# Key-value sums in 32-column strips and a new order of all jobs, in a one-core linear-attention and mixer kernel

## The chip, the core and the metric

The program runs on one core of one Trainium2 chip. The core has TensorE (PE), VectorE (DVE), ScalarE (ACT), GpSimd (POOL) and SyncE (SP), each with its own instruction stream; they meet through semaphores. PE reads SBUF and writes PSUM, which here is one tile `banks` of eight banks of 512 float32 columns. The metric is the device time of one execution in microseconds (us), as the median of several runs.

## What is computed

With x of 2048 tokens and 448 features, everything in bfloat16 and xn = layernorm(x), the output is x + A(xn) + B(xn).

```
q, k, v = split(xn @ wqkv)               # 16 heads of 28
pq, pk  = q @ w_phi, k @ w_phi           # per head
phi_q   = concat(softmax(pq), softmax(-pq));  phi_k the same of pk
kv, z   = phi_k^T @ v, sum_s phi_k       # per head, over all tokens
A = (phi_q @ kv) / (phi_q @ z + 1e-6) @ wo
h = gelu(layernorm(xn) @ w1); four column groups of h shifted by +1, -1, +2, -2 tokens
x1 = xn + shifted(h) @ w2
B = x1 + gelu(layernorm(x1) @ w3) @ w4
```

## The kernel before, in words

**Recording and order.** Nothing is issued while the Python code runs. `Recorder` (from L19) collects every operation with the memory that it reads and writes; `solve` (L76) works out which semaphore each must wait for, and `emit` plays one list per engine. All matmuls have the line L204, all ScalarE operations L212, most VectorE and GpSimd operations L216. So the order on each engine is the order of the calls, and that is written out by hand in two lists: the jobs of `chain` (L960 to L981) and the pairs of `play` (L1046 to L1068).

**Tiling.** There are 16 token tiles of 128 tokens. The 448 features are cut into overlapping chunks, so that most matmuls use 64 rows of the array. Lower rows (0 to 63, `LO`) and upper rows (64 to 127, `HI`) hold different weights and write different banks; `row_pairs` (L530) interleaves one of each. A matmul of 64 rows and 128 weight columns is in the profile as 64*128, its moving operand as, for example, 64x448. `Recorder._tile` (L198) notes the row division; on a change of division `solve` makes PE wait for its own last matmul on the same bank.

**The chain (prologue).** Layernorm statistics on VectorE (`"m"`), the inverse root on ScalarE (`"q"`) or GpSimd (`"r"`), the apply on VectorE (`"a"`) or GpSimd (`"p"`), PE transposes of xn (`XT`, L208), value projections (`ZV`), w1 products (`ZW`, `ZH`), the leftover columns of w1 (`ZR`), the folding of w_phi into w_qkv (`FO`), and dummy matmuls on a constant (`HD`, `spin`). `chain` (L562) plays the lower half of each job at once and puts the upper half into a queue that follows 400 columns behind. A "zip" job gives one half four chunks and the other three; `odd` alternates which. At its end stand the first key, query and w2 products (`HF`).

**The list after it.** `k0`/`k1` and `q0`/`q1` are the key and query projections of two token tiles (two PE halves each) with ScalarE exponentials behind; `kn` is `k_norm` (a VectorE reduction and a reciprocal), `kx` is `k_product` (the GpSimd product of phi_k, L723). `w0`/`w1_` are the w2 products, with VectorE additions behind (`w2_out`). `lo`, `sc`, `A` and `G` are the second layernorm: statistics on VectorE, scale on GpSimd, apply (`g_apply`, on VectorE for the tiles in `on_dve`, else on GpSimd) and a DMA transpose on SP's queue into gT. `T` is the DMA transpose of the query exponentials; `a`/`b` are the two PE halves of a w3 pair (eight and six matmuls of 512 columns) with a Gelu behind that writes h3T, which lies over phi_k. `N` is the attention product of a tile with its VectorE and GpSimd division, `f` the four parts of the last products, `S` the store.

**Key-value sums.** `K` is `kv_tile` (L725): 16 matmuls a tile, eight pairs of a lower and an upper half, weights a block of phi_k (64 tokens by 128 columns), moving 59 columns of `vaug` (values with a column of ones); lower halves add up in bank 6 and upper halves in bank 7. `kv_copy` (L739) copies bank 6 and adds bank 7; `kv_blocks` (L744) gathers the diagonal blocks with four matmuls against the selection matrix `pick` and four copies of 32 partitions, two on VectorE and two on ScalarE, into `kvq`, which `num_tile` (L766) reads as moving operand.

Of the kernel before, what the change touches and what calls it, by code (L numbers as in the profile page):

```python
# [224 lines left out]
def bass_parallel_sum__linear_kernel_hedgehog__mixer_s_mlp__prompt_kernel(  # L225
# [17 lines left out]
    with es:  # L243
# [58 lines left out]
        kvT = view(w1_r, 512)  # L302
        kvf = view(w1_r, 512, F32, at=1024)
        pick = view(w1_r, 2 * 128, at=3072).rearrange("p (s c) -> p s c", s=2)
# [257 lines left out]
        def chain(jobs, lag, even):  # L562
            at, upper, seen = [0, 0], deque(), {}
            odd, left = False, sum(j[0] == "zip" for j in jobs)
# [37 lines left out]
            for kind, make, then, *mid in jobs:  # L602
# [12 lines left out]
                else:  # L615
                    for n, item in enumerate(make(LO, (0, 1, 3) if odd else (0, 1, 2, 3))):
                        if mid and n == mid[0][0]:
                            both(*mid[0][1][1:])
                        low(item)
# [3 lines left out]
                    left -= 1  # L623
                    odd = not odd and left > even
# [281 lines left out]
        fb = {(1, 0): 3, (1, 2): 1, (0, 0): 3, (0, 2): 1}  # L906
# [45 lines left out]
        def HF(p, n):  # L952
# [7 lines left out]
        chain([  # L960
            L(("m", 0), ("q", 0, 1)), do(load_wT, 0, (1, 2, 3)), L(("m", 1), ("q", 1, 1), ("a", 0), ("a", 1)), HD(3, 3),
            HD(6, 3), HD(3, 3), L(("m", 2)), XT(0, 0, 1, "ACT"), L(("q", 2, 1)), HD(6, 3), L(("m", 3), ("m", 4)),
            XT(1, 2, 1, "ACT"), L(("p", 2), ("q", 3, 1), ("q", 4, 1), ("a", 3)), HD(6, 3), HD(6, 3), ZV(0, EV(0, "ACT", 1)),
            L(("m", 5), ("m", 7)), ZV(1, EV(1, "ACT", 1)), XT(2, 4, 1, "ACT"), L(("p", 4)), ZH(2, 0),
            L(("q", 5, 1), ("p", 5), ("m", 6), ("r", 6, 1)), inside(1, ZH(1, 0), XT(3, 0, 1, "ACT")), ZV(2, EV(2, "ACT", 1)),
            L(("q", 7, 1)), inside(1, ZH(0, 0), XT(4, 0, 1, "ACT")), L(("a", 7)),
            inside(2, ZH(0, 1, EW(0, 0, 1)), XT(5, 6, 1, "2")), L(("m", 15)), inside(1, ZH(2, 1), XT(7, 0, 1, "DVE")),
            L(("p", 6), ("m", 14), ("r", 15, 1)), ZV(3, EV(3, "ACT", 1)), ZV(4, EV(4, "ACT", 1)),
            inside(2, ZH(1, 1, EW(0, 1, 2)), XT(6, 0, 1, "DVE")), L(("m", 12), ("r", 14, 1), ("m", 13), ("a", 14)),
            ZV(5, EV(5, "ACT", 1)), ZW(1, 0, EW(1, 0, 1)), L(("p", 15), ("r", 12, 1), ("a", 12), ("m", 8)),  # L970
            ZW(1, 1, EW(1, 1, 1)), ZW(1, 2, EW(1, 2, 1)), L(("r", 13, 1)), XT(12, 6, 1, "ACT"), XT(14, 2, 2, "DVE"),
            L(("p", 13), ("m", 11)), do(load_w2), L(("r", 8, 1), ("p", 8)), ZV(7, EV(7, "ACT", 1)), L(("m", 10)),
            ZV(6, EV(6, "ACT", 1)), L(("m", 9), ("r", 11, 1), ("r", 10, 1)), XT(13, 6, 1, "ACT"), ZV(15, EV(15, "ACT", 1)),
            L(("a", 11)), do(phi_blocks), L(("a", 10)), ZV(14, EV(14, "ACT", 1)), ZW(3, 0, EW(3, 0, 1)),
            ZV(13, EV(13, "ACT", 1)), XD(11), XD(10), XT(8, 3, 1, "2"), FO(1, 2, 0), ZW(3, 2, EW(3, 2, 1)), FO(1, 0, 0),
            do(load_w3, 0), FO(1, 2, 1), ZW(3, 1, EW(3, 1, 1)), L(("r", 9, 1)), FO(1, 0, 1), ZV(12, EV(12, "ACT", 1)),
            ZV(8, EV(8, "ACT", 1)), L(("p", 9)), inside(3, ZR(0, 6, (rest_out, 0, 6), (rest_T, 0)), XT(9, 3, 1, "2")),
            FO(0, 2, 0), FO(0, 0, 0), FO(0, 2, 1), FO(0, 0, 1), ZV(9, EV(9, "DVE", 1)), do(late_3), do(h_shift, 0),
            ZR(1, 5, (rest_out, 1, 5)), do(kv_ones), ZV(11, EV(11, "ACT", 1)), HF(0, 0), ZW(2, 2, EW(2, 2, 1)), do(load_w4),
            ZW(2, 1, EW(2, 1, 1)), ZW(2, 0, EW(2, 0, 1)), ZV(10, EV(10, "DVE", 1)), HF(0, 1), HF(2, 0), HF(1, 0), HF(2, 1),  # L980
            do(h_shift, 1), do(kv_picks), HF(1, 1), do(rest_T, 1)], 400, 0)  # L981

        on_dve = (6, 8, 12)
# [42 lines left out]
        def A(i):  # L1026
            g_apply(i, dve if i in on_dve else pool)
# [75 lines left out]
```

## Time and profile before

| what | value |
|---|---|
| median of 3 runs | 171.19 us (171.19 to 171.23) |
| span of the profiled execution, first to last instruction | 169.2 us |
| what lies around it (median less span; the profiled execution's own total is not recorded) | 1.99 us |
| PE busy, matmuls | 165.9 us, 2359 |
| VectorE, GpSimd, ScalarE busy | 109.6, 92.2, 82.1 us |
| granted TensorE clock | 1.000 |

The span is the time between the first and the last instruction of the program. Busy times are those of the engines' instructions; a matmul's end is modelled, so that its duration contains the depth of the pipeline, and only the distance between starts tells how fast matmuls follow one another.

### The profile page before, as it was taken

Reading aid. Unit: us, or ns where it says so; the run is one execution under the profiler, and the core shown is the slowest. Engines: PE = TensorE matmul, PEld = TensorE weight load, DVE = VectorE, ACT = ScalarE, POOL = GpSimd, SP = SyncE. Lnnn points to the kernel's source line nnn. Section 1 sums busy time; section 2 is a strip of 40 time slices with the busy share of each in tenths; the row PEclk is TensorE's granted clock in tenths of the full one; section 3 lists DMA queues with packets and bytes.
Section 4 is the critical chain, followed back from the end, with each engine's and each line's share of the span. In section 5 each row is a group of like instructions: output and inputs, shape, how many; then the busy total and the mean of one; then the engine's idle time right before and its main releaser. Section 6 shows DMA issues by size and latency. Waiting matters only on the chain.

```text
span 169.2 us, 5423 instructions
## 1 busy us (share of the span) xinstructions
PE 165.9 (98%) x2359; PEld 99.3 (59%) x2359; DVE 109.6 (65%) x248; ACT 82.1 (49%) x110; POOL 92.2 (54%) x124
## 2 busy tenths in 40 slices
PE   8999999999999999999999999999999999999994
PEld 7776778667786555554554555555545555444453
DVE  3998866159999899929685896718617586220031
ACT  3599975797998878646242422024204041144000
POOL 5288980005999999951792264396730845404040
PEclk9999999999999999999999999999999999999999
DMA  5995579999599985671076664434554422310031
GB/s 162 364 197 103 98 135 293 164 330 149 99 141 183 278 97 149 86 134 27 7 118 127 95 135 55 84 73 42 135 68 93 59 61 62 83 60 4 0 109 54
DMA packets 50567, 19.93 MB, mean 118 GB/s; under 512 B 41712, under 2 KB 49840, under 8 KB 50544
## 3 DMA queue, kind: packets, MB, share of 16 engines
q1 hardware_dynamic: 49424, 18.71, 57.1%
q10 hardware_dynamic: 1120, 0.89, 1.6%
q8 instruction: 18, 0.29, 0.8%
q14 instruction: 5, 0.04, 0.1%
HBM read 7.14 MB, written 1.84 MB: 53 GB/s over the span
## 4 chain that ended last, share of the span: by engine, by line
PE 95%; DMA 1%; DVE 1%; issue 0%; DVEq 0%
PE banks L204 94%; DMA xtok<-in_A_x_dram 1%; PE banks L208 1%; DVE st L216 1%; DVE mv L216 0%; DVE xn L216 0%; DVE vaug L216 0%; DVEq L166 0%
## 5 line engine op out<-in xcount | busy, mean ns | idle before, releaser
L212 ACT ACTIVATE phik<-banks 128x1024 bf16<-128x1024 f32 (+1 forms) x44 | 42.2, 987 | 60.7 <-PE banks L204 60.5
L216 DVE TENSOR_TENSOR vaug<-banks,vaug 128x464 f32<-128x464 f32 (+3 forms) x65 | 32.8, 513 | 26.1 <-PE banks L204 24.5
L204 PE MATMUL banks<-gT,w 64*128 64x512 bf16 x392 | 48.2, 376 | 0.0
L204 PE MATMUL banks<-w,phik 64*128 64x448 bf16 (+3 forms) x434 | 45.2, 343 | 0.0
L216 POOL TENSOR_TENSOR xnT<-vaug 128x196 bf16<-128x196 f32 (+1 forms) x32 | 18.1, 587 | 29.6 <-DVE vaug L216 29.6
L204 PEld LDWEIGHTS banks<-w,phik 64*128 64x128 bf16 (+1 forms) x434 | 22.3, 94 | 20.1 <-issue 0.4
L204 PE MATMUL banks<-wv,xnT 64*128 64x448 bf16 (+2 forms) x222 | 32.9, 346 | 0.0
L723 POOL TENSOR_TENSOR phik<-phik,rks 128x1792 bf16<-128x1792 bf16 x8 | 25.6, 3219 | 8.5 <-DVE rks L216 8.5
L204 PEld LDWEIGHTS banks<-gT,w 64*128 64x128 bf16 x392 | 17.9, 94 | 18.0 <-ACT phik L212 0.4
L216 POOL TENSOR_TENSOR vaug<-xn,xtok 128x448 f32<-128x448 bf16 x16 | 16.2, 1034 | 12.7 <-DVE vaug L216 12.7
L204 PEld LDWEIGHTS banks<-wv,xnT 64*128 64x128 bf16 (+1 forms) x222 | 14.0, 94 | 7.7 <-PE banks L204 0.3
L204 PE MATMUL banks<-xnT,w 64*128 64x512 bf16 (+1 forms) x105 | 16.6, 334 | 0.0
L204 PE MATMUL banks<-wpk,xnT 64*128 64x448 bf16 x112 | 16.6, 349 | 0.0
L216 DVE TENSOR_REDUCE ksum<-phik 128x64 f32<-128x1792 bf16 x8 | 16.0, 2000 | 0.0
L204 PE MATMUL banks<-wpq,xnT 64*128 64x448 bf16 x112 | 15.7, 349 | 0.0
L212 ACT ACTIVATE hi<-banks 128x896 bf16<-128x896 f32 x16 | 13.7, 923 | 2.0 <-PE banks L204 2.0
L204 PE MATMUL banks<-w,hT 64*128 64x448 bf16 x96 | 13.6, 349 | 0.0
L216 POOL TENSOR_TENSOR rs<-mv,mhalf 128x1 f32<-128x1 f32 (+1 forms) x13 | 9.4, 727 | 6.2 <-DVE mv L216 6.0
L216 DVE RECIPROCAL vaug<-banks 128x16 f32<-128x16 f32 x16 | 4.0, 250 | 12.6 <-PE banks L204 12.6
L216 DVE TENSOR_TENSOR xn<-banks,xn 128x512 bf16<-128x512 f32 (+1 forms) x16 | 8.9, 598 | 2.3 <-PE banks L204 2.3
L216 POOL TENSOR_SCALAR g_tok<-xn,rs 128x512 bf16<-128x512 bf16 x13 | 9.9, 774 | 0.2
L216 DVE BATCH_NORM_STATS2 st<-xtok 128x6 f32<-128x448 bf16 x16 | 9.6, 601 | 0.2 <-DMA xtok<-in_A_x_dram 0.2
(67 smaller groups left out, 172.7 us busy)
## 6 DMA issues: line engine op xcount, KB each, us to landing
w<-in_B_w_dram SPq DMA_DIRECT2D x2, 896.0 KB, 5.8
out_dram<-vaug SPq DMA_DIRECT2D x15, 112.0 KB, 1.8
w<-in_B_w_dram SPq DMA_DIRECT2D x1, 1568.0 KB, 8.6
xtok<-in_A_x_dram SPq DMA_DIRECT2D x2, 448.0 KB, 6.3
wv<-in_A_wo_dram SPq DMA_DIRECT2D x2, 224.0 KB, 3.3
xtok<-in_A_x_dram SPq DMA_DIRECT2D x3, 112.0 KB, 3.6
xtok<-in_A_x_dram ACTq DMA_DIRECT2D x3, 112.0 KB, 4.2
w<-in_B_w_dram SPq DMA_DIRECT2D x1, 336.0 KB, 4.1
```

The lines of the kernel that those rows point to most:

```text
L204: self.op("PE", lambda e: e.matmul(out, lhsT, rhs, start=start, stop=stop, skip_group_check=True), [out], [lhsT, rhs], tile=self._tile(lhsT))
L208: self.op("PE", lambda e: e.transpose(out, in_, ident), [out], [in_, ident], tile=self._tile(in_))
L212: self.op("ACT", lambda e: e.activation(out, in_, func, **kw), [out], [in_] + aps)
L216: self.op(eng, lambda e: getattr(e, name)(out, *args, **kw), [out], aps)
L723: R.op(pool, lambda e: e.tensor_tensor(ph, ph, wide, op=ALU.mult), [ph], [ph, wide, *after])
```

## The change

The key-value sums change sides: `vaug` (30 columns of a head, all 128 tokens) becomes the weights and 64 columns of phi_k the moving operand. Each matmul's output lies in one of four strips of 32 PSUM partitions, which names one of four 32-column strips of the array. There are again 16 matmuls a tile, all in bank 6. One VectorE transpose in 32x32 blocks (`kv_turn`) and one product with a 0/1 mask (`kv_blocks`) then make `kvq`; the four gathering matmuls and the copies go. The 16 tiles are summed in five groups with no other PE work inside: (0, 4), (2, 5), (1, 3, 7, 11), (12, 13, 6, 10), (14, 8, 9, 15).

In `chain` a string of digits now tells for each zip job which half gets four chunks (1: the upper). The banks of value and w1 products are re-assigned and both lists are written anew. `AD` is the second layernorm's apply on VectorE, `A` on GpSimd. w2 is loaded at the front of the chain, the first half of w3 at its end, and wo just behind it. In the lists below only the new side is shown; the old one stands in the kernel above.

```diff
-        kvT = view(w1_r, 512)
-        kvf = view(w1_r, 512, F32, at=1024)
-        pick = view(w1_r, 2 * 128, at=3072).rearrange("p (s c) -> p s c", s=2)
+        kvT = view(w1_r, 256, F32)
+        pick = new("pick", 2, F32)
-        def chain(jobs, lag, even):
+        def chain(jobs, lag, heavy):
             at, upper, seen = [0, 0], deque(), {}
-            odd, left = False, sum(j[0] == "zip" for j in jobs)
+            turns = iter(heavy)
...
+                    odd = next(turns) == "1"
...
-                    left -= 1
-                    odd = not odd and left > even
...
         def kv_tile(i):
-            def side(k, rows):
-                return [(banks[6 + k][:, 64 * n:64 * n + VP + DH + 1],
-                         phik[rows[0]:rows[1], i, 4 * n:4 * n + 4, :].rearrange("p g e -> p (g e)"),
-                         vaug[rows[0]:rows[1], i, 2 * VP * n:2 * VP * n + VP + DH + 1]) for n in range(8)]
-            row_pairs(side(0, LO), side(1, HI), i == 0)
+            for n in range(4):
+                for j in range(4):
+                    h = 8 * (j // 2) + 2 * n + j % 2
+                    R.mm(banks[6][HP * j:HP * j + VP, 64 * n:64 * n + 64], vaug[:, i, VP * h:VP * h + VP],
+                         phik[:, i, 2 * h:2 * h + 2, :].rearrange("p g e -> p (g e)"), i == 0 and n == 0, False)
 
         def kv_picks():
-            R.ew(pool, "memset", pick[:, :, :], 0.0)
+            R.ew(pool, "memset", pick[:, :], 0.0)
             for q in range(4):
-                r = slice(HP * q, HP * q + HP)
-                R.ew(dve, "tensor_copy", pick[r, q % 2, :].rearrange("p (n e) -> p n e", n=4),
-                     ident[r, HP * q:HP * q + HP].unsqueeze(1).to_broadcast([HP, 4, HP]))
-
-        def kv_copy():
-            n61 = [a.rearrange("p (n e) -> p n e", n=8)[:, :, 0:VP + DH + 1] for a in (banks[6], banks[7], kvf, kvT)]
-            R.ew(dve, "tensor_copy", n61[2], n61[0])
-            R.ew(dve, "tensor_tensor", n61[3], n61[1], n61[2], op=ALU.add)
+                R.ew(dve, "memset", pick[HP * q:HP * q + HP, q % 2:q % 2 + 1], 1.0)
+
+        def kv_turn():
+            R.ew(dve, "transpose", kvT[:, :], banks[6][:, 0:256])
 
         def kv_blocks():
-            kt = kvT.rearrange("p (n e) -> p n e", n=8)
-            for s in range(2):
-                for k, lo in enumerate((0, 64)):
-                    R.mm(banks[6 + k][:, 256 * s:256 * s + 256].rearrange("p (n e) -> p n e", n=8)[:, :, 0:DH + 1],
-                         pick[lo:lo + 64, s, :], kt[lo:lo + 64, :, VP * k:VP * k + DH + 1], s == 0, False)
-            for q in range(4):
-                r, h, n = slice(HP * q, HP * q + HP), q % 2, 4 * (q // 2)
-                src = banks[6 + h][r, :].rearrange("p (s n e) -> p s n e", s=2, n=8)[:, :, n:n + 4, 0:DH + 1]
-                dst = kvq[r, :, VP * h:VP * h + DH + 1].rearrange("p (c s) e -> p s c e", s=2)
-                if h:
-                    R.act(dst, src, ACT.Copy)
-                else:
-                    R.ew(dve, "tensor_copy", dst, src)
+            R.ew(dve, "tensor_tensor", kvq[:, :, 0:2 * VP].rearrange("p b (h e) -> p b h e", h=2)[:, :, :, 0:DH + 1],
+                 kvT.rearrange("p (b e) -> p b e", e=HP)[:, :, 0:DH + 1].unsqueeze(2).to_broadcast([128, 8, 2, DH + 1]),
+                 pick.unsqueeze(1).unsqueeze(3).to_broadcast([128, 8, 2, DH + 1]), op=ALU.mult)
...
-        vb = {0: 6, 1: 7, 2: 5, 3: 6, 4: 5, 5: 7, 6: 4, 7: 1, 8: 0, 9: 7, 10: 1, 11: 0, 12: 7, 13: 0, 14: 5, 15: 3}
-        gb = ((4, 2, 3), (1, 0, 5), (5, 6, 4), (7, 5, 6))
+        vb = {0: 6, 1: 7, 2: 5, 3: 6, 4: 5, 5: 7, 6: 4, 7: 0, 8: 0, 9: 1, 10: 7, 11: 7, 12: 7, 13: 0, 14: 5, 15: 1}
+        gb = ((4, 2, 3), (1, 0, 5), (0, 2, 3), (7, 5, 6))
...
+            L(("m", 0)), HD(5, 3), do(load_wT, 0, (1, 2, 3)), do(load_w2), L(("q", 0, 1)), L(("m", 1)), L(("a", 0)),
+            HD(5, 3), L(("q", 1, 1)), HD(3, 3), L(("a", 1)), HD(5, 3), HD(0, 3), L(("m", 2)), XT(0, 3, 1, "ACT"),
+            HD(1, 3), L(("m", 3)), L(("q", 2, 1)), XT(1, 1, 1, "ACT"), L(("m", 4)), L(("p", 2)), L(("q", 3, 1)),
+            L(("a", 3)), ZV(0, EV(0, "ACT", 1)), L(("m", 5)), L(("m", 7)), L(("m", 6)), ZV(1, EV(1, "ACT", 1)),
+            L(("q", 4, 1)), XT(2, 4, 1, "ACT"), ZH(2, 0), L(("q", 5, 1)), L(("p", 4)),
+            inside(1, ZH(1, 0), XT(3, 0, 1, "ACT")), L(("p", 5)), ZV(2, EV(2, "ACT", 1)), L(("q", 7, 1)), L(("a", 7)),
+            inside(1, ZH(0, 0), XT(4, 0, 1, "ACT")), L(("r", 6, 1)), L(("m", 15)),
+            inside(2, ZH(0, 1, EW(0, 0, 1)), XT(5, 6, 1, "2")), L(("p", 6)), L(("r", 15, 1)), L(("p", 15)),
+            inside(1, ZH(2, 1), XT(7, 0, 1, "DVE")), ZV(3, EV(3, "ACT", 1)), L(("m", 14)), ZV(4, EV(4, "ACT", 1)),
+            inside(2, ZH(1, 1, EW(0, 1, 2)), XT(6, 0, 1, "DVE")), L(("m", 12)), ZV(5, EV(5, "ACT", 1)),
+            L(("r", 14, 1)), L(("m", 13)), L(("a", 14)), L(("r", 12, 1)), L(("m", 8)), L(("m", 11)), L(("p", 12)),
+            ZW(1, 1, EW(1, 1, 1)), ZW(1, 0, EW(1, 0, 1)), ZW(1, 2, EW(1, 2, 1)), XT(14, 2, 2, "DVE"),
+            XT(12, 6, 1, "ACT"), L(("m", 10)), L(("r", 13, 1)), L(("p", 13)), L(("r", 8, 1)), L(("m", 9)),
+            ZV(6, EV(6, "ACT", 1)), do(phi_blocks), ZV(7, EV(7, "ACT", 1)), XT(13, 6, 1, "ACT"),
+            ZV(15, EV(15, "ACT", 1)), L(("r", 10, 1)), L(("r", 11, 1)), L(("a", 11)), L(("a", 8)),
+            ZV(14, EV(14, "ACT", 1)), L(("a", 10)), ZW(3, 0, EW(3, 0, 1)), ZV(13, EV(13, "ACT", 1)), XD(11),
+            XT(8, 3, 1, "DVE"), FO(1, 2, 0), ZW(3, 2, EW(3, 2, 1)), L(("r", 9, 1)), do(late_3), FO(1, 0, 0),
+            L(("a", 9)), FO(1, 2, 1), ZW(3, 1, EW(3, 1, 1)), FO(1, 0, 1), ZV(12, EV(12, "DVE", 1)), XD(10),
+            ZV(8, EV(8, "ACT", 1)), inside(3, ZR(0, 6, (rest_out, 0, 6), (rest_T, 0)), XT(9, 3, 1, "2")), FO(0, 2, 0),
+            FO(0, 0, 0), ZR(1, 5, (rest_out, 1, 5)), FO(0, 2, 1), FO(0, 0, 1), do(h_shift, 0),
+            ZV(10, EV(10, "ACT", 1)), do(kv_ones), do(kv_picks), ZW(2, 0, EW(2, 0, 1)), do(load_w4),
+            ZW(2, 1, EW(2, 1, 1)), ZW(2, 2, EW(2, 2, 1)), ZV(11, EV(11, "DVE", 1)), ZV(9, EV(9, "DVE", 1)),
+            do(h_shift, 1), do(rest_T, 1), HF(0, 0), HF(2, 0), HF(1, 0), do(load_w3, 0), HF(0, 1), HF(2, 1), HF(1, 1)], 400,
+            "110001010101101001010100111010100")
...
-        on_dve = (6, 8, 12)
...
-            g_apply(i, dve if i in on_dve else pool)
+            g_apply(i)
+
+        def AD(i):
+            g_apply(i, dve)
...
+            (kn, 0), (w0, 2), (k0, 1), (w1_, 2), (k1, 1), (kx, 0), (k0, 2), (q0, 1), (wo_in,), (T, 1), (k1, 2),
+            (q1, 1), (kn, 1), (q0, 2), (T, 2), (lo, 0), (kx, 1), (k0, 3), (q1, 2), (w0, 4), (kn, 2), (k1, 3),
+            (w1_, 4), (kn, 3), (q0, 3), (k0, 4), (T, 0), (lo, 2), (q1, 3), (T, 3), (k1, 4), (T, 4), (w0, 6), (q0, 4),
+            (w1_, 6), (kx, 2), (T, 5), (lo, 1), (lo, 3), (kx, 3), (q1, 4), (K, 0), (K, 4), (sc, 0), (A, 1), (k0, 5),
+            (K, 2), (T, 6), (T, 7), (K, 5), (load_w3, 1), (k1, 5), (kn, 4), (q0, 5), (G, 1), (A, 3), (w0, 8), (q1, 5),
+            (k0, 6), (G, 3), (w1_, 8), (AD, 0), (k1, 6), (A, 2), (q0, 6), (w0, 10), (kn, 5), (G, 2), (q1, 6), (k0, 7),
+            (w1_, 10), (lo, 5), (lo, 7), (k1, 7), (lo, 6), (kx, 4), (lo, 4), (w0, 12), (q0, 7), (kx, 5), (G, 0),
+            (w1_, 12), (q1, 7), (sc, 4), (kn, 6), (a, 0), (K, 1), (K, 3), (AD, 4), (K, 7), (kn, 7), (K, 11), (b, 0),
+            (a, 1), (AD, 5), (w0, 14), (AD, 7), (b, 1), (w1_, 14), (a, 2), (lo, 11), (a, 3), (A, 6), (b, 2), (lo, 10),
+            (kx, 6), (kx, 7), (b, 3), (G, 4), (K, 12), (lo, 14), (K, 13), (lo, 8), (K, 6), (K, 10), (a, 4), (a, 5),
+            (b, 4), (G, 6), (lo, 12), (b, 5), (K, 14), (K, 8), (K, 9), (K, 15), (kc,), (lo, 9), (sc, 8), (G, 5),
+            (a, 6), (G, 7), (a, 7), (kb,), (T, 9), (AD, 8), (AD, 9), (b, 6), (b, 7), (N, 1), (f, 1, 0), (T, 10),
+            (N, 0), (a, 8), (T, 8), (T, 11), (a, 9), (b, 8), (AD, 11), (G, 8), (lo, 15), (b, 9), (A, 10), (N, 3),
+            (f, 2, 0), (N, 2), (lo, 13), (a, 10), (a, 11), (b, 10), (f, 3, 0), (b, 11), (G, 11), (G, 9), (f, 4, 0),
+            (G, 10), (a, 12), (N, 4), (a, 13), (sc, 12), (A, 14), (f, 1, 1), (T, 14), (A, 12), (b, 13), (N, 6),
+            (S, 0), (f, 3, 1), (b, 12), (f, 2, 1), (N, 5), (a, 14), (S, 1), (A, 13), (a, 15), (b, 14), (f, 4, 1),
+            (G, 12), (b, 15), (G, 14), (G, 13), (N, 8), (A, 15), (a, 16), (f, 1, 2), (S, 3), (b, 16), (a, 17),
+            (f, 3, 2), (a, 18), (N, 7), (f, 2, 2), (f, 4, 2), (S, 4), (G, 15), (b, 17), (b, 18), (T, 13), (N, 9),
+            (f, 1, 3), (a, 19), (f, 3, 3), (b, 19), (S, 2), (N, 10), (a, 20), (f, 2, 3), (f, 4, 3), (S, 5), (T, 15),
+            (a, 21), (b, 20), (S, 7), (N, 11), (f, 1, 4), (f, 3, 4), (T, 12), (b, 21), (N, 13), (S, 6), (f, 2, 4),
+            (a, 23), (f, 4, 4), (a, 22), (b, 23), (N, 15), (b, 22), (f, 1, 5), (N, 12), (f, 3, 5), (a, 24), (a, 25),
+            (N, 14), (b, 24), (b, 25), (f, 2, 5), (f, 4, 5), (S, 11), (a, 27), (S, 9), (a, 26), (b, 27), (b, 26),
+            (S, 8), (f, 1, 6), (f, 2, 6), (fin_tails,), (S, 10), (f, 3, 6), (S, 12), (S, 13)])
```

More of the change, by code (lines that the diff above doesn't have):

```diff
@@ L904, in ln1 @@
                     ln1_apply(pool if op == "p" else dve, *n)
-        fb = {(1, 0): 3, (1, 2): 1, (0, 0): 3, (0, 2): 1}
+        fb = {(0, 0): 3, (0, 2): 1, (1, 0): 3, (1, 2): 1}
         def do(f, *args):
@@ L955, in HF @@
             return "half", halves_of(*head[p][n], n == 0), then
-        vb = {0: 6, 1: 7, 2: 5, 3: 6, 4: 5, 5: 7, 6: 4, 7: 1, 8: 0, 9: 7, 10: 1, 11: 0, 12: 7, 13: 0, 14: 5, 15: 3}
-        gb = ((4, 2, 3), (1, 0, 5), (5, 6, 4), (7, 5, 6))
+        vb = {0: 6, 1: 7, 2: 5, 3: 6, 4: 5, 5: 7, 6: 4, 7: 0, 8: 0, 9: 1, 10: 7, 11: 7, 12: 7, 13: 0, 14: 5, 15: 1}
+        gb = ((4, 2, 3), (1, 0, 5), (0, 2, 3), (7, 5, 6))
         spin(30)
         chain([
[L961 to L981, printed above, removed]
@@ L1043, in wo_in @@
             load_lap(wo, A_wo, (eng, eng))
[L1045 removed]
+        K, G, S, T, kc, kb, W = kv_tile, g_T, store, q_T, kv_turn, kv_blocks, fin_tails
         play([
[L1047 to L1068 removed]
```

23 lines of the change are left out of this document (removed).

## The prediction

> **What bounds the kernel now.** I read the page first: the span, the busy shares, and the chain that ended last.
>
> ```profile
> span 169.2 us, 5423 instructions
> PE 165.9 (98%) x2359; PEld 99.3 (59%) x2359; DVE 109.6 (65%) x248; ACT 82.1 (49%) x110; POOL 92.2 (54%) x124
> PE 95%; DMA 1%; DVE 1%; issue 0%; DVEq 0%
> ```
>
> TensorE (PE) is busy 98% of the span and the chain of work runs through it for 95%. A busy PE need not be streaming at its peak, so the second view is the waits: what PE ever stood still for. Its weight loads (PEld) show it.
>
> ```profile
> PEld banks L204 <- issue: 1.4, 3, 0.8
> PEld banks L204 <- PE banks L204: 0.9, 3, 0.3
> PEld banks L204 <- ACT phik L212: 0.6, 3, 0.2
> PEld banks L204 <- DVE w L216: 0.5, 1, 0.5
> PEld banks L208 <- DVE xn L216: 0.3, 1, 0.3
> PEld banks L208 <- POOL rs L216: 0.3, 1, 0.3
> ```
>
> The columns are total us, times, longest. All of it is some 4 us of 169. The third view is PE's timeline, whose starts tell the pace. Here is the stretch with the last key-value sums and the step that rearranges them.
>
> ```profile
> 71.34 0.62 PE L204 MATMUL banks<-vaug,phik 64*128 64x59 bf16 x32
> 71.80 1.67 PE L204 MATMUL banks<-gT,w 64*128 64x512 bf16 x14
> 73.31 0.62 PE L204 MATMUL banks<-vaug,phik 64*128 64x59 bf16 x32
> 73.77 1.67 PE L204 MATMUL banks<-gT,w 64*128 64x512 bf16 x14
> 75.27 0.62 PE L204 MATMUL banks<-vaug,phik 64*128 64x59 bf16 x32
> 75.73 1.67 PE L204 MATMUL banks<-gT,w 64*128 64x512 bf16 x14
> 77.39 0.39 PE L204 MATMUL banks<-w 64*128 64x232 bf16 x4
> 77.60 1.68 PE L204 MATMUL banks<-gT,w 64*128 64x512 bf16 x14
> ```
>
> Read starts, not the durations beside them, which contain the pipeline's depth. From 71.80 to 73.31, 14 matmuls of 512 columns take 1.51 us, so two of them, one in each row half, take 0.216 us: the halves run side by side and a pair costs its columns. From 71.34 to 71.80, 32 matmuls of 59 columns (two token tiles) take 0.46 us, 14.4 ns each or 29 ns a pair. There is no gap between groups. The kernel after its first few microseconds is therefore a sum of column counts, and **an edit is worth what it takes off PE's stream**, as long as the other engines keep up. Stage by stage (us, then busy PE, PEld, DVE, ACT, POOL):
>
> ```profile
> 34.00:50.00 16.00, 16.00 (x182) 11.83 (x179) 14.10 (x19) 14.61 (x19) 9.62 (x3) 1.00 0.93 177
> 50.00:62.00 12.00, 12.00 (x224) 7.37 (x217) 11.24 (x20) 9.88 (x12) 11.70 (x9) 1.00 0.93 196
> 62.00:77.40 15.40, 15.40 (x276) 8.09 (x271) 12.04 (x22) 10.17 (x11) 11.94 (x8) 1.00 0.72 118
> 77.40:100.00 22.60, 22.60 (x310) 11.73 (x310) 17.66 (x50) 8.37 (x11) 11.36 (x18) 1.00 0.43 77
> ```
>
> From 34 to 62 us VectorE (DVE) and GpSimd (POOL) are nearly as full as PE (11.24 and 11.70 of 12.00). This is where a faster PE may find something late; after 77 us there is room.
>
> **The change part by part.**
>
> *Key-value sums.* Before: 16 token tiles of 16 matmuls, 64 rows by 128 columns of weights, 59 moving. At 0.46 us for two tiles that is 8 x 0.46 = 3.68 us of PE. After: again 16 matmuls a tile, but each uses all 128 token rows, 30 weight columns in one of four 32-column strips, and 64 moving columns. Four consecutive matmuls go to four strips. No matmul in this trace uses a strip, so the cost is bounded by the nearest rows, a run of 64-column matmuls in two row halves:
>
> ```profile
> 16.40 0.51 PE L208 MATMUL banks<-ident,xn 64*128 64x64 bf16 x24
> 16.75 0.38 PE L204 MATMUL banks<-xnT,w 64*128 64x512 bf16 x1
> ```
>
> 24 of them in 0.35 us is 29 ns for a pair. If four strips stream side by side as two row halves do, four matmuls take those 29 ns: 4 x 29 x 16 = 1.86 us. If only two proceed at a time (14.5 ns a matmul, the pace of these rows), 3.7 us; if none overlap, 29 ns each, 7.4 us. Below 1.86 us nothing can go, since a strip's own columns must pass. I take 1.86, because the row halves in this trace overlap without loss and consecutive matmuls always name another strip: **-1.82 us**. The Trainium skill, "TensorE: Matmul & The Clock Gate", section "Part 3: Packing small matmuls — row/col tiling", gives 2.38 times for three column strips at 512 columns, short of three; by an estimate from that page the four strips would take 2.3 us and the sum below would end 0.5 us later. No run here shows it.
>
> *Changes of shape.* The strips stand in five groups (2, 2, 4, 4 and 4 tiles) among 64-row matmuls, so PE changes the array's division ten times. The trace has one such change while streaming, near the end, from 64-row pairs to 128-row matmuls:
>
> ```profile
> 156.88 2.82 PE L204 MATMUL banks<-w,phik 64*128 64x448 bf16 x28
> 159.54 0.73 PE L204 MATMUL banks<-wv,xnT 64*128 64x448 bf16 x6
> 160.20 1.12 PE L204 MATMUL banks<-w,phik 128*128 128x448 bf16 x5
> ```
>
> Fourteen pairs take 159.54 - 156.88 = 2.66 us, 0.19 each; the next three should take 0.57 and take 0.66. So 0.09 us is lost, and I take 0.1 for each change: **+1.0 us**. The bounds are nothing (the row halves alternate without a gap) and 0.19 a change (the whole modelled length of a 59-column matmul, if it had to end before the next could begin):
>
> ```profile
> L204 PE MATMUL banks<-vaug,phik 64*128 64x59 bf16 x256 | 5.5, 187 | 0.0
> ```
>
> so 0 to 1.9 us.
>
> *Rearranging the sums.* `kv_copy` and `kv_blocks` go with their four PE matmuls. Those take 77.60 - 77.39 = 0.21 us, and the 14 matmuls before them 1.66 where the same 14 took 1.50 after 73.77, so PE also stood still 0.16 us: **-0.37 us**. What replaces them is on VectorE alone: one transpose of 128x256 read from PSUM and one product of 464 results. Their nearest rows:
>
> ```profile
> 75.93 0.65 DVE L216 COPY w<-banks 128x472 f32<-128x472 f32 x1 [3.01 <-PE banks L204]
> 76.68 0.65 DVE L216 TENSOR_TENSOR w<-banks,w 128x472 bf16<-128x472 f32 x1
> 78.01 0.76 DVE L216 CAST kvq<-banks 32x232 bf16<-32x232 f32 x2
> ```
>
> Two instructions of about 0.65 us take the place of 0.65 + 0.65 + 0.76. Between the last sum and the first attention tile that needs the result stand (a,6), (a,7), (b,6), (b,7): 28 matmuls of 512 columns, 2 x 1.51 = 3.0 us of PE, while VectorE has the transpose, one set of statistics and the product, under 2.2 us. Hidden, with 0.8 us to spare; if the cover went, the price would be what exceeds 3.0. ScalarE loses two small copies.
>
> *Row halves of the prologue.* In the chain each job gives one half four chunks and the other three. Counted from the lists (448 columns for a value tile, 512 or 256 for w1 jobs, 512 for the rest jobs), the lower half had 50,304 columns and the upper 50,048; now 50,048 and 50,304. The folds and the head's key and query jobs give the lower half more in both versions, so the lower half ends later, and 256 columns at 0.19 us per 448 are **-0.11 us**. It is worth nothing if the upper half's lag, not the lower's length, ends the chain.
>
> *Order, banks and engines.* Every wait of PE quoted above, without the last rearrangement's 0.5, is about 3.5 us, much of it before the first data are there. A better order could win some of it, a worse one could add as much; I take zero and keep -0.7 to +0.7. Loads are moved too, all on SP's queue:
>
> ```profile
> w<-in_B_w_dram SPq DMA_DIRECT2D x2, 896.0 KB, 5.8
> wv<-in_A_wo_dram SPq DMA_DIRECT2D x2, 224.0 KB, 3.3
> 64.17 1.02 PE L204 MATMUL banks<-gT,w 64*128 64x512 bf16 x8
> ```
>
> The first half of w3 (896 KB, 5.8 us from issue to landing) goes from the chain's middle to its end, before the stage that begins at 34, and PE first uses it at 64.17. The reload of wo (two of 3.3 us) goes from beside that use to just behind the chain, ahead of the query transposes; those have to land before their buffer comes round eight token tiles later, or before attention. w2 goes to the front, behind the x, w1 and transposed w_qkv loads, so it delays none of these. I cost the moves at nothing. Four of the second normalization's applies before the last key sum move from POOL to VectorE while one moves back:
>
> ```profile
> L216 DVE TENSOR_SCALAR g_tok<-xn,mv,rs 128x512 bf16<-128x512 bf16 x3 | 1.3, 424 | 0.8 <-POOL rs L216 0.8
> L216 POOL TENSOR_SCALAR g_tok<-xn,rs 128x512 bf16<-128x512 bf16 x13 | 9.9, 774 | 0.2
> 67.71 6.42 POOL L723 TENSOR_TENSOR phik<-phik,rks 128x1792 bf16<-128x1792 bf16 x2
> ```
>
> POOL gets 3 x 0.77 = 2.3 us of room ahead of its last key products, VectorE 3 x 0.42 = 1.3 us more work. The last product ended at 67.71 + 6.42 = 74.13, and PE came for it at 75.27: 1.14 us to spare. Ahead of that first tile of the last group PE formerly had 14 tiles (3.2 us); now it has 12 (1.4 us) and nine changes of shape (0.9), and 0.1 less prologue, but also one more half of a w3 pair (six matmuls, three pairs of 0.216, 0.65 us). It comes 0.4 us earlier than before, inside the room. So I cost the moved applies at nothing; without that room, each 0.1 us is paid in full.
>
> **Sum.** -1.82 - 0.37 - 0.11 + 1.0 = -1.3 us. The profiled execution's span of 169.2 becomes 167.9. The median of the runs shown, 171.19, has 1.99 us around that span; this stays: 169.9 us.
>
> **Rivals.**
>
> *Weight loads set the pace (ends slower).* Every key-value matmul loads its own weights. The trace shows two loads in 29 ns and never more; four strips in 29 ns need four. If loads pass at the pace of the quoted rows, four matmuls take 58 ns, the sums still cost 3.7 us, and the changes of shape are pure loss: +1.0 - 0.48 = +0.5, **171.7 us**. The sign turns at 49 ns for four (64 x 49 = 3.15 us), and it is measurably slower from about 55. At its far end, nothing overlapping, 7.4 us: +4.3, 175.5 us. For it: nothing here shows four at once. Against: 59-column pairs are at their column count, so the loads were not yet the limit. The Trainium skill, "TensorEngine Tiling (Array Packing)", section "Restrictions and Gotchas", says that column tiling excludes Fast Weight Load, which speaks for this rival; no run here shows it.
>
> *Something else is late (a smaller gain).* PE arrives early at key products, exponentials or statistics that VectorE and POOL finish no sooner than before. Their shares from 34 to 62 us speak for it, the 1.14 us of room against. It would give back about two thirds of the gain: **170.8 us**.
>
> *The new order also heals the prologue.* The early ones among the waits quoted shrink by 0.7 us in all: **169.2 us**. For it: the chain now fixes job by job which half is longer. Against: the first 8 us are a chain of load, statistics, apply and transpose that no order shortens.
>
> **How the numbers follow.** Forecast 0.44 at 169.9 (its own range 169.3 to 170.6); healed prologue 0.09; something late 0.17, of which 0.07 is still faster by over 0.2%, 0.06 within, 0.04 slower; loads at two a pair 0.20, of which 0.05 within and 0.15 slower; no overlap 0.10. Together faster 0.60, same 0.11, slower 0.29; 0.2% (0.34 us) is about what a measurement of this kernel can tell from no change. The range, 169.0 to 172.0, takes in the healed prologue and loads at two a pair with changes of 0.1 us, and leaves out the far end.
>
> **What would show it.** Right: 16 matmuls of 64 columns start within 0.12 to 0.13 us; a gap near 0.1 us beside each of ten borders; the four matmuls at 77.39 and the stop before them gone; 512-column groups still at 0.216 us a pair. Wrong: strip matmuls that start 14 ns apart or more; borders of 0.15 us or more; PEld waits on phik or gT that were not there; POOL's products ending after PE comes for them.

## The result and the profile after

The changed kernel is **slower**: a median of 177.92 us (four runs, 175.40 to 179.32) beside 171.19 us (four runs, 171.03 to 171.23), a ratio of 1.0292 with an interval of 1.0230 to 1.0355. The ratio is not the quotient of the two medians, as it leaves out runs at a mean granted TensorE clock of 0.981 (two of these four, one of another kernel below); what lowered the clock is part of the explanation. The profiled execution took 175.40 us at a clock of 1.000, with a span of 173.7 us: 4.5 us more than before, where 1.3 less was forecast.

The same rows of the page as before, span, busy times and the chain that ended last:

```profile
span 173.7 us, 5401 instructions
PE 165.6 (95%) x2355; PEld 110.4 (64%) x2355; DVE 116.2 (67%) x252; ACT 79.7 (46%) x106; POOL 88.1 (51%) x118
PE 81%; DVE 9%; POOL 5%; DMA 3%; issue 1%; ACTq 0%; ACT 0%
```

PE's busy time hardly moved (165.9 to 165.6), the span grew by 4.5: PE stands still. The chain now runs 9% through VectorE and 5% through GpSimd, which had 1% and nothing. VectorE is busy 6.6 us longer with four instructions more. The waits of after (engine, line, what it waited for: us in total, times, longest) say where:

```profile
PEld banks L204 <- DVE xn L216: 2.9, 2, 2.6
PEld banks L208 <- DVE xn L216: 2.8, 2, 2.5
PE banks L204 <- DVE xn L216: 2.2, 1, 2.2
PE banks L208 <- DVE xn L216: 2.1, 1, 2.1
```

Two stops, each of them listed twice (weight load and matmul), and both put down to a VectorE result. The first, on PE's timeline (start, duration, matmuls, and in brackets the idle time before):

```profile
20.85 0.35 PE L204 MATMUL banks<-wv,xnT 64*128 64x448 bf16 x1
23.28 0.29 PE L208 MATMUL banks<-ident,xn 64*128 64x64 bf16 x8 [2.08 <-DVE xn L216]
```

A matmul of 448 columns is over 0.19 us after its start, so PE streams nothing from 21.04 to 23.28, 2.24 us. It waits to transpose a normalized tile. VectorE and GpSimd at that time:

```profile
19.87 3.66 DVE L216 TENSOR_SCALAR xn<-xtok,mv,rs 128x512 bf16<-128x512 bf16 x3 [0.44 <-POOL rs L216]
20.31 1.80 POOL L434 MEMSET phik<- 128x2048 bf16 x1
22.05 0.52 POOL L216 MEMSET kvq<- 128x512 bf16 x1
22.51 0.52 POOL L216 MEMSET hi<- 128x512 bf16 x1
```

Three applies (tiles 11, 8 and 10) take 3.66 us. In the trace the second starts 0.33 us behind the first and lasts 3.02, from 20.20 to 23.22: as long as GpSimd's three fills (20.31 to 23.03) run, and it ends just behind them. In the chain before, GpSimd itself made the applies of tiles 8 and 9 (`p`), and only then its fills (`late_3`), when VectorE's last apply was over; VectorE, then GpSimd:

```profile
20.45 0.41 DVE L216 TENSOR_SCALAR xn<-xtok,mv,rs 128x512 bf16<-128x512 bf16 x1
...
21.27 0.77 POOL L216 TENSOR_SCALAR xn<-xtok,rs 128x512 bf16<-128x512 bf16 x1
21.98 1.81 POOL L435 MEMSET phik<- 128x2048 bf16 x1
```

The new chain gives both applies to VectorE (`a`) and calls the fills right behind GpSimd's last scale. In the written list three of the four applies still stand ahead of the fills, but nothing makes GpSimd wait for them, and it reaches the fills at 20.31.

The second stop, 63.87 to 66.21, 2.34 us, in the stage of the key sums; PE, then VectorE, then GpSimd:

```profile
63.68 0.35 PE L204 MATMUL banks<-w,hRT 64*128 64x448 bf16 x2
66.21 0.93 PE L204 MATMUL banks<-wpq,xnT 64*128 64x448 bf16 x8 [2.18 <-DVE xn L216]
...
59.63 3.00 DVE L216 TENSOR_SCALAR g_tok<-xn,mv,rs 128x512 bf16<-128x512 bf16 x1
62.55 2.01 DVE L216 TENSOR_REDUCE ksum<-phik 128x64 f32<-128x1792 bf16 x1
64.59 0.55 DVE L216 RECIPROCAL rks<-ksum 128x64 f32<-128x64 f32 x1
65.06 1.09 DVE L216 TENSOR_TENSOR xn<-banks,xn 128x512 bf16<-128x512 f32 x2
...
59.27 3.21 POOL L721 TENSOR_TENSOR phik<-phik,rks 128x1792 bf16<-128x1792 bf16 x1
```

`(AD, 0)`, one of the four applies moved to VectorE, takes 3.00 us: it ends 0.15 us behind the key product `(kx, 4)` on GpSimd, which ends at 62.48. Behind it on VectorE stand a reduction, a reciprocal and the additions that empty PE's banks; these end at 66.15, and PE goes on at 66.21.

The group of the second layernorm's applies on VectorE, for the row of 424 ns in the prediction:

```profile
L216 DVE TENSOR_SCALAR g_tok<-xn,mv,rs 128x512 bf16<-128x512 bf16 x7 | 6.1, 889 | 1.2 <-POOL rs L216 1.2
```

And the strips. PE's timeline of after, two groups of two tiles and one of four:

```profile
52.81 0.42 PE L204 MATMUL banks<-phik,vaug 128*30 128x64 bf16 x32
53.16 0.93 PE L204 MATMUL banks<-wpk,xnT 64*128 64x448 bf16 x8
...
80.05 0.69 PE L204 MATMUL banks<-phik,vaug 128*30 128x64 bf16 x64
80.67 3.20 PE L204 MATMUL banks<-gT,w 64*128 64x512 bf16 x28
```

From the start of a group to the start of what follows, 32 of them cost 0.35 us and 64 cost 0.62. Inside a group the 64 start within 0.49 us, 7.7 ns apart, 31 ns for four: they overlap four at a time. What is left of the 0.35 and 0.62 is the change of shape behind the group (its border), 0.10.

### The profile page after: what moved, and what is told of

The parts are those of the page before. It is cut to its first block, busy times and chain, and to the rows that moved or that the text cites. A ratio compares the mean times of both kernels' runs of the same rounds, so it can differ in the third digit from the quotient of the medians.

```text
span 173.7 us, 5401 instructions
## 1 busy us (share of the span) xinstructions
PE 165.6 (95%) x2355; PEld 110.4 (64%) x2355; DVE 116.2 (67%) x252; ACT 79.7 (46%) x106; POOL 88.1 (51%) x118
## 4 chain that ended last, share of the span: by engine, by line
PE 81%; DVE 9%; POOL 5%; DMA 3%; issue 1%; ACTq 0%; ACT 0%
PE banks L204 81%; DVE xn L216 3%; POOL rs L216 3%; DMA xtok<-in_A_x_dram 3%; POOL xn L216 2%; DVE g_tok L216 2%; DVE st L216 2%; DVE ksum L216 1%; DVE mv L216 1%; DVE rks L216 0%; ACTq L222 0%; ACT L365 0%; PE banks L208 0%; DVE vaug L216 0%
## 5 line engine op out<-in xcount | busy, mean ns | idle before, releaser
L204 PE MATMUL banks<-w,phik 64*128 64x448 bf16 (+3 forms) x434 | 45.9, 343 | 0.0
L204 PEld LDWEIGHTS banks<-w,phik 64*128 64x128 bf16 (+1 forms) x434 | 31.3, 94 | 10.5 <-issue 0.4
L204 PE MATMUL banks<-wv,xnT 64*128 64x448 bf16 (+2 forms) x222 | 34.7, 346 | 0.5 <-ACT xnT L212 0.5
L216 POOL TENSOR_TENSOR xnT<-vaug 128x280 bf16<-128x280 f32 (+1 forms) x32 | 18.1, 587 | 31.9 <-DVE vaug L216 31.9
L204 PEld LDWEIGHTS banks<-gT,w 64*128 64x128 bf16 x392 | 23.9, 94 | 14.4 <-ACT phik L212 0.8
L204 PEld LDWEIGHTS banks<-wv,xnT 64*128 64x128 bf16 (+1 forms) x222 | 16.3, 94 | 6.2 <-ACT xnT L212 1.0
L204 PE MATMUL banks<-wpq,xnT 64*128 64x448 bf16 x112 | 14.2, 349 | 2.2 <-DVE xn L216 2.2
L204 PE MATMUL banks<-wpk,xnT 64*128 64x448 bf16 x112 | 14.5, 350 | 0.0
L204 PE MATMUL banks<-w,hT 64*128 64x448 bf16 x96 | 12.5, 349 | 0.0
L204 PEld LDWEIGHTS banks<-wpq,xnT 64*128 64x128 bf16 x112 | 5.9, 94 | 7.3 <-DVE xn L216 2.6
(63 smaller groups left out, 165.9 us busy)
```

The source lines that it names most:

```text
L204: self.op("PE", lambda e: e.matmul(out, lhsT, rhs, start=start, stop=stop, skip_group_check=True), [out], [lhsT, rhs], tile=self._tile(lhsT))
L216: self.op(eng, lambda e: getattr(e, name)(out, *args, **kw), [out], aps)
```

## The experiments

**Theory.** A VectorE apply (SBUF to SBUF, `TENSOR_SCALAR`) stands still while GpSimd is inside an instruction that uses SBUF; it was moved to places where GpSimd is in a long one (fills of 2.8 us, products of 3.2 us), and PE waits for what stands behind it. **Rivals.** The strips or their borders cost PE more than the stops show; or the re-ordered jobs are late in themselves, so that PE would wait at the same places for something else if the applies were quick. Times are medians; before had 171.08 to 171.14 us on the three chips of the experiments, and a ratio is estimated from the single runs, to before on the same chip, and need not be the quotient of the medians.

**Each stop by itself, and both.** The first is removed by moving the fills behind the last apply of the chain, and letting the first fill wait for the applies of tiles 8 to 11:

```diff
-            ... L(("r", 9, 1)), do(late_3), FO(1, 0, 0), L(("a", 9)), FO(1, 2, 1), ...
+            ... L(("r", 9, 1)), FO(1, 0, 0), L(("a", 9)), do(late_3), FO(1, 2, 1), ...
-            R.op(pool, lambda e: e.memset(pad, 0.0), [pad], [xn[:, NT - 2, :]])
+            R.op(pool, lambda e: e.memset(pad, 0.0), [pad], [xn[:, 8:12, :]])
```

> Changed kernel; only GpSimd's three fills of late_3 move behind the VectorE applies of tiles 8, 9 and 10 (they wait for these). Theory (a VectorE apply and a GpSimd instruction exclude one another): the apply that took 3.0 us takes 0.4, PE's stop of 2.2 us before the transposes of tile 8 goes, the span falls from 173.7 to about 171.5; the second stop near 64 to 66 us stays at 2.3 us. Rival (VectorE simply has too much work there, or the apply waits for its statistics): the stop stays within 0.5 us of 2.2 and the span stays at 173.5 or more.

Measured: 174.55 us (173.28 to 175.50, six runs), 1.0198 (1.0157 to 1.0240). VectorE and GpSimd of this kernel at the same place:

```profile
20.11 1.06 DVE L216 TENSOR_SCALAR xn<-xtok,mv,rs 128x512 bf16<-128x512 bf16 x3 [0.44 <-POOL rs L216]
...
22.41 1.80 POOL L434 MEMSET phik<- 128x2048 bf16 x1 [1.81 <-DVE xn L216]
```

The same three applies take 1.06 us instead of 3.66. The two runs at full clock, 173.28 and 173.39, stand 2.1 us below the profiled 175.40.

The second stop is removed by letting the key product wait for the apply:

```diff
-            k_product(2 * n, [g_tok[:, :, :]] if n == 7 else [])
+            k_product(2 * n, {4: [g_tok[:, 0, :]], 7: [g_tok[:, :, :]]}.get(n, []))
```

> Changed kernel; only GpSimd's product kx 4 now waits for the apply of tile 0, which stays on VectorE at its place. Theory (exclusion): that apply takes 0.4 us in place of 3.0, PE's stop of 2.3 us at 63.9 goes, the span falls by about 2.2 us to 171.5 although GpSimd's product starts 0.8 us later; the first stop at 21 us stays. Rival (too much VectorE work): VectorE has the same work, so the stop stays near 2.3 us and the span near 173.7.

Measured: 174.89 us (172.92 to 177.81, four runs), 1.0171 (1.0100 to 1.0243). VectorE, then GpSimd:

```profile
61.62 0.40 DVE L216 TENSOR_SCALAR g_tok<-xn,mv,rs 128x512 bf16<-128x512 bf16 x1
61.94 2.01 DVE L216 TENSOR_REDUCE ksum<-phik 128x64 f32<-128x1792 bf16 x1
...
62.11 6.38 POOL L721 TENSOR_TENSOR phik<-phik,rks 128x1792 bf16<-128x1792 bf16 x2 [0.82 <-DVE g_tok L216]
```

The apply takes 0.40 us, GpSimd loses 0.82 us of waiting, and the stop at 64 is gone. The reduction, now with a product beside it nearly all along, still takes 2.01: it isn't held up. The only run at full clock took 172.92 us, 2.5 below 175.40.

> Changed kernel with both edits. Theory: both stops go, span about 169.2 to 169.6, time about 171.0, and the runs no longer differ by some us, with a granted clock of 1.00 in all of them, if the lost clock of the slower runs came from PE's stops. Rival: 174 to 175 us, spread as before.

Measured with both edits: **171.26 us** (170.94 to 171.90, ten runs), 1.0003 (0.9982 to 1.0024), as expected. Of the profiled 175.40 the two stops were 4.1 us. That settles it against the second rival at these two places: nothing else was late behind the applies.

**A lower clock behind a stop.** The clock of 1.00 came back in all ten runs of this kernel (0.999 to 1.000), while with one stop left it was 0.99 or less in four of six and three of four runs. The profile with the first stop left (the second removed) caught it. Its stretches (us; busy PE, PEld, DVE, ACT, POOL; granted clock; DMA share, GB/s), with the stop in the first row:

```profile
20.00:23.50 3.50, 1.54 (x16) 0.76 (x12) 3.28 (x3) 1.53 (x4) 3.42 (x6) 1.00 0.74 174
23.50:27.00 3.50, 3.38 (x45) 2.34 (x47) 1.96 (x5) 0.98 (x2) 0.00 (x0) 0.52 0.42 93
27.00:30.00 3.00, 3.00 (x80) 2.36 (x76) 2.08 (x4) 1.72 (x4) 0.00 (x0) 0.99 0.24 56
```

Right after a stop of 2.1 us (the 2.08 before 23.62 in its timeline) PE gets 0.52 of its clock for 3.5 us: 3.5 x 0.48 = 1.7 us more, nearly the price of the stop again. One such stretch in 173 us is a mean clock of 0.990, two are 0.980, about the clocks of the three longer runs of after (0.990, 0.981, 0.981). The distance from 175.40 to the median of 177.92 fits this loss, once or twice an execution. The stretch itself was seen in one profile only, and one stop does not always mean one stretch: the slowest run with the first stop left, 177.81 us, had 0.981 too, and the profiled execution of after had both stops and lost no clock.

**The same fault put into the kernel before.** `late_3` alone moved ahead of the last applies:

```diff
-            ... L(("m", 9), ("r", 11, 1), ("r", 10, 1)), XT(13, 6, 1, "ACT"), ... do(late_3), do(h_shift, 0), ...
+            ... L(("m", 9), ("r", 11, 1), ("r", 10, 1)), do(late_3), XT(13, 6, 1, "ACT"), ... do(h_shift, 0), ...
```

> Kernel before, with only the three GpSimd fills of late_3 issued ahead of the VectorE applies of tiles 11 and 10 in place of behind them. Theory (exclusion of a two-port VectorE operation and a GpSimd instruction): one of these applies takes 2 to 3 us in place of 0.4, PE stops for it, the time rises by 1 to 2.5 us to 172 to 173.7. Rival: fills and applies run side by side, within 0.3 us of 171.2.

Measured: 173.18 us (173.02 to 173.42), 1.0123 (1.0104 to 1.0142), 2.1 us slower. VectorE, then GpSimd:

```profile
19.93 2.85 DVE L216 TENSOR_SCALAR xn<-xtok,mv,rs 128x512 bf16<-128x512 bf16 x1
...
19.90 1.80 POOL L435 MEMSET phik<- 128x2048 bf16 x1
21.65 0.53 POOL L216 MEMSET kvq<- 128x512 bf16 x1
22.11 0.52 POOL L216 MEMSET hi<- 128x512 bf16 x1
```

One apply of 2.85 us, from the first fill to the end of the third: VectorE does not get in between fills that follow one another. PE was idle for 1.86 us before 23.13; in none of these four runs did the clock fall (0.999 to 1.000).

**The strips by themselves.** The kernel before with the strip sums, `kv_turn` and the new `kv_blocks`, its own chain, and its `K` jobs gathered into four groups:

```diff
+    (0, 4) | (2, 3, 1, 7, 5) | (6, 11, 10) | (8, 9, 12, 13, 15, 14)     # K tiles, no other PE job inside
```

> Kernel before with nothing but the key-value sums in 32-column strips, in four groups (2, 5, 3 and 6 tiles), with the transpose and the masked product behind. Theory of the prediction with the sizes measured in the changed kernel (16 tiles of 0.123 us, eight borders of 0.097, the gather's 0.37 gone): 3.68 us of sums become 2.75, total -1.3 us, 169.9 us. Rival (the strips themselves are what made the changed kernel slow, by stops that the trace assigns to others): 172 us or more.

Measured: 172.08 us (171.61 to 172.82, ten runs), 1.0049 (1.0027 to 1.0070): a miss of 2.2 us. PE's timeline:

```profile
65.05 1.04 PE L204 MATMUL banks<-gT,w 64*128 64x512 bf16 x8 [0.52 <-DMA gT<-g_tok]
...
70.86 5.17 PE L204 MATMUL banks<-gT,w 64*128 64x512 bf16 x42
75.96 0.95 PE L204 MATMUL banks<-phik,vaug 128*30 128x64 bf16 x96
```

42 matmuls of 512 columns are 21 pairs of 0.216 us, 4.54; with a border of 0.10 the sums should start 4.64 us later, and start 5.10 later. In the trace PE twice stops for 0.23 us between the two halves of a w3 pair (four times in all, 0.9 us), and the waits name PE's own last matmuls:

```profile
PEld banks L204 <- PE banks L204: 3.3, 7, 0.6
```

Before, this row had 0.9 us and three times. The `K` jobs had stood between `a` and `b` of a pair and covered that wait. And with the sums gone from ahead of it, PE reaches the first w3 product at 64.5, before its DMA transpose has landed, and waits 0.52 us. These are 1.4 of the 2.2 us; the rest was not taken apart. The order with the strips was not free to choose.

The same, with every `K` left where it stood (ten groups):

> Kernel before with the strips and nothing else moved: the tiles stay where they stood, in ten groups, so PE changes shape twenty times and every key-value tile still stands between the two halves of a w3 pair. Theory (border 0.097 us each, tile 0.123 us): 16 x 0.123 + 20 x 0.097 = 3.9 us for 3.68, less 0.37 for the gather: -0.15 us, 171.0 us, and none of the 0.23 us stops between halves of a w3 pair that the four-group version showed. Rival (the stops of the four-group version come from the strips, not from the lost spacers): the stops stay and the time is 172 us or more.

Measured: 171.79 us (171.13 to 172.88), 1.0037 (1.0012 to 1.0062). 19 of the 20 borders cost 0.09 to 0.10 us in the trace, and one, ahead of the first w3 product, 0.21; that is 2.0 us and eats what the strips win. That explains no gain; the 0.8 us above the expectation it doesn't. Most of it is one stop in the stage of the first key, query and w2 products, for a DMA transpose that the kernel before did not wait for:

```profile
33.90 0.35 PE L204 MATMUL banks<-w,hT 64*128 64x448 bf16 x1
...
34.62 0.35 PE L204 MATMUL banks<-w,hRT 64*128 64x448 bf16 x1 [0.37 <-DMA hRT<-gT]
```

PE streams nothing from 34.09 to 34.62, 0.53 us. Ahead of this place the edit changes only how `pick` is filled, and whether the DMA is late in every execution of this kernel or by chance in this one stays open.

**The old chain with the new list.** Before's `chain`, banks and alternation of halves; the new second list and the repaired key product:

> Chain, banks and alternation of the kernel before; strips, five groups and the second list of the changed kernel, with GpSimd's product kx 4 behind the apply of tile 0. By the lower half's idle time up to 40 us (1.33 us in the kernel before, 2.50 in the changed kernel with both stops removed), the new prologue costs 1.2 us: theory 171.26 - 1.2 = 170.1 us. Rival (the new prologue's idle time is only shifted, and the second list would wait anyway): 171.0 us or more.

Measured: 170.70 us (170.33 to 171.95, ten runs), 0.9984 (0.9964 to 1.0004), 0.6 us above the expectation. By medians the new prologue without its stop thus costs 171.26 - 170.70 = 0.6 us, half of what was expected of it; the ratios (1.0003 and 0.9984, each give or take 0.002) make it 0.3 us, give or take 0.5, so that it is likely but not shown. Then three further applies (tiles 8, 9 and 11), which the change has on VectorE ahead of the attention's divisions, went to GpSimd; before had tile 8 on VectorE as well:

```diff
-            ... (T, 9), (AD, 8), (AD, 9), (b, 6), ... (AD, 11), (G, 8), ...
+            ... (T, 9), (A, 8), (A, 9), (b, 6), ... (A, 11), (G, 8), ...
```

> As e7_old_chain_new_list, and the applies of tiles 8, 9 and 11 are GpSimd's again, so that VectorE's attention divisions do not stand behind them. Theory: PE's stops of 0.12 and 0.18 us at the first attention tiles go, 169.8 us. Rival: GpSimd becomes late instead, 170.1 us or more.

Measured: **170.58 us** (170.08 to 170.86, ten runs), **0.9963 (0.9949 to 0.9977)**: faster than the kernel before by a third of a per cent, 0.8 us above the expectation, of which 0.6 us are those of the run before, on which it was built. The two stops at the first attention tiles went, as expected: from the first to the second attention product PE takes 2.87 us in place of 2.98, from the third to the fourth 2.87 in place of 3.04. By medians the edit is worth 0.12 us, less than these runs tell apart. The group of applies is back to

```profile
L216 DVE TENSOR_SCALAR g_tok<-xn,mv,rs 128x512 bf16<-128x512 bf16 x4 | 1.8, 477 | 0.0
```

**One border less, and the sums themselves.** In the last kernel, tiles 0 and 4 joined to 2 and 5:

```diff
-            ... (q1, 4), (K, 0), (K, 4), (sc, 0), (A, 1), (k0, 5), (K, 2), (T, 6), ...
+            ... (q1, 4), (sc, 0), (A, 1), (k0, 5), (K, 0), (K, 4), (K, 2), (T, 6), ...
```

> As e8_and_late_applies_on_pool, with the first two groups joined behind k0 5: (0, 4, 2, 5), so two changes of shape fewer. Theory (each change costs 0.097 us and nothing else hangs on the place of the first group): -0.19 us, 170.4 us where e8 gave 170.58; the trace shows eight borders and no new stop. Rival (the first group also gave ScalarE time to empty a bank for k0 5): PE stops there instead, 170.6 us or more.

Measured: 170.90 us (170.14 to 171.53, eleven runs), 0.9965 (0.9936 to 0.9995), where the kernel without this edit had 170.58 and 0.9963: no gain. PE's timeline shows why:

```profile
50.30 0.80 PE L204 MATMUL banks<-wpq,xnT 64*128 64x448 bf16 x6
51.32 0.93 PE L204 MATMUL banks<-wpk,xnT 64*128 64x448 bf16 x8 [0.22 <-ACT phik L212]
52.18 0.69 PE L204 MATMUL banks<-phik,vaug 128*30 128x64 bf16 x64
```

Three pairs of 0.19 us end their streaming at 50.87, and the next product starts at 51.32: 0.45 us of waiting, more than the two borders saved. The first group had covered ScalarE's exponentials, which empty the bank that the key product needs. And the kernel of 170.58 us with the old sums and gather in the same places:

> As e8_and_late_applies_on_pool, but with the key-value sums, the copies and the gathering matmuls of the kernel before: the strips alone taken out. Theory (strips worth 3.68 - 3.0 = 0.65 us with their ten borders, the gather 0.37): 170.58 + 1.0 = 171.6 us. Rival (the second list, not the strips, is what makes e8 faster): within 0.3 us of 170.6.

Measured: 171.31 us (170.93 to 173.44, eleven runs), 1.0012 (0.9983 to 1.0041). Strips and gather together are worth 171.31 - 170.58 = 0.7 us in place, 0.8 by the ratios, give or take 0.5, where 1.0 was expected.

## Why the prediction was wrong, point by point

**PE sets the pace: right.** Each stop of PE taken away came off the time about in full (2.1 and 2.5 us alone, 4.1 together, for stops of 2.24 and 2.34).

**Key-value sums: mechanism and size right.** Four strips take 31 ns where 29 was forecast. With their ten borders the sums take 2 x 0.350 + 3 x 0.620 us, and five borders into a group at 0.093: 3.03 us for 3.68, -0.65 where -1.82 + 1.0 = -0.82 stood. The rival of the weight loads falls: they pass four at a time. One argument against it was misread, though: at 0.216 us for 512 columns, 59 columns are 25 ns, so the old pairs at 29 ns were not at their column count. The estimate of 2.3 us that the prediction drew from the Trainium skill, "TensorE: Matmul & The Clock Gate", section "Part 3: Packing small matmuls — row/col tiling", is too long as well: the pace inside the groups is 256 x 7.7 ns = 2.0 us, nearer to the 1.86 of the sum.

**Changes of shape: right.** 0.093 us into a strip group and 0.10 out of it, for 0.1 forecast.

**The gather: right.** Transpose and masked product took 0.40 and 0.60 us (0.65 each forecast) and lay beside the w3 products, as the timeline of after shows: the attention product at 83.70 follows its predecessors without a gap.

```profile
81.09 0.40 DVE L216 STREAM_TRANSPOSE w<-banks 128x256 f32<-128x256 f32 x1
82.16 0.60 DVE L216 TENSOR_TENSOR kvq<-w,pick 128x464 bf16<-128x464 f32 x1
83.70 0.38 PE L204 MATMUL banks<-kvq,eqT_lo 64*128 64x60 bf16 x16
```

In sum the two were to bring 1.2 us; the trace has 1.0 and the medians 0.7.

**Row halves: open.** 0.11 us is less than these runs tell apart, and the experiments took the levelling and the new chain together.

**Order, banks and engines: the step that failed.** It said "VectorE 3 x 0.42 = 1.3 us more work" and "I cost the moved applies at nothing", and kept 0.7 us to either side. The 0.42 came from a group of three applies beside none or little of GpSimd's long work. The right price was the remaining length of GpSimd's work: 2.85 us left of a product made an apply of 3.00 us, 2.83 us left of the fills one of 3.02. The step looked for room on GpSimd, which had it, and not on VectorE, which was busy 11.24 of 12.00 us in that stage by the rows that the prediction quotes; 2.6 us more in it had to end on PE. And the prologue's applies and fills were not looked at, although the diff moves the applies of tiles 8 and 9 from GpSimd to VectorE and `late_3` to an earlier place. The trace of before had a sign of it: its one apply between 62 and 77 us, and what ran on GpSimd then:

```profile
67.36 0.54 DVE L216 TENSOR_SCALAR g_tok<-xn,mv,rs 128x512 bf16<-128x512 bf16 x1
65.48 2.27 POOL L216 TENSOR_SCALAR g_tok<-xn,rs 128x512 bf16<-128x512 bf16 x3
```

It ends 0.15 us behind GpSimd's (67.90 and 67.75), and is the longest of the three. The rule that explains it is in the Trainium skill, "SBUF — State Buffer", section "Who interferes with whom": VectorE's second pair of SBUF ports is also GpSimd's, copies, casts and `tensor_scalar` can take both pairs, the pair is locked for a whole instruction and the other engine waits until it is free, while `tensor_reduce` never contends. The traces agree on each count: 0.40 us alone and 3.00 beside a product of 3.21, the reduction 2.01 in both. It is the rule that spoke against this change, and the prediction weighed two others. Only one thing goes beyond it: the lock passed over three fills in a row without VectorE getting in.

**The rivals.** "Something else is late" had the place of the second stop's cause, VectorE and GpSimd from 34 to 62 us, but not of the first, at 21 us, and a price of two thirds of the gain where 4.1 us were due, because it too thought of arrival times and not of instructions that grow. "The new order heals the prologue" went the other way: by medians 0.6 us slower without the stop, which is at the edge of what the runs tell apart; which of the moved jobs does that wasn't taken apart. What no case held is the clock: after a stop of 2.1 to 2.3 us PE could lose another 1.7. And the 1.99 us around the span mixed two executions: 175.40 and 173.7 are 1.7 apart, as are time and span of the other runs within 0.1, so that the forecast stood some 0.25 us too high from the start.

**The balance**, by medians: sums and gather -0.7, the rest of the new list against before +0.2, late applies on VectorE +0.1, new prologue +0.6, two stops +4.1, clock +2.5. Together +6.8 for the measured 177.92 - 171.19 = 6.7; each term is the distance between two neighbouring kernels (175.40, one execution, stands for the stops without the lost clock), so the sum must come out and confirms nothing. The stops, the clock and the -0.7 are clear of the noise, the +0.2 and +0.1 are not.

## What to carry to other kernels

Price a copy or `tensor_scalar` moved to VectorE, or a GpSimd instruction moved past one, by GpSimd's timeline at its new place: it can last until GpSimd's long instruction, or an unbroken row of short ones, is over, and a near-full VectorE hands all of it on. A job that looks free to move may be what covers a wait (PE's own last matmuls, ScalarE emptying a bank), so look at what stands on both sides of it before gathering. And where PE never stops, the first stop of 2 us can cost nearly as much again in clock.

## What was not expected of the hardware

In the profile that caught it, the granted clock was 0.52 over the 3.5 us behind a stop of only 2.1 us; the mean clock was lowered in 10 of the 14 executions with such stops, and in none of the four with the stop of 1.9 us that the fills put into the kernel before. The Trainium skill, "TensorE: Matmul & The Clock Gate", section "HAM oscillation — how this bites in real kernels", puts the limit at idle gaps over about 3.4 us; the trace shows a shorter one. Matmuls of 64 columns in four strips started 7.7 ns apart, each with weights of its own, and a change between row halves and strips while streaming cost 0.09 to 0.10 us in the timelines above, but for the one of 0.21 ahead of a first w3 product.
